# A new order of loads, units and fillers for the first batch of a fused retention and Fourier-mixing kernel

## The chip, the cores and the metric

The kernel runs on one core of a Trainium2 chip. The metric is the device time of one execution in microseconds (us). The names of the engines follow the profile: PE is TensorE, DVE is VectorE, ACT is ScalarE, POOL is GpSimd, SP is SyncE, which only issues DMAs here.

## What is computed

Cut to what matters:

```python
# q, k, v: (4, 8, 768, 64); gamma_h = 1 - 2**(-5 - h)
for t in range(768):                       # retention, for each batch and head
    state = gamma * state + outer(k[t], v[t])
    y[t] = (1 / 8) * q[t] @ state
x = y of all 8 heads side by side          # (4, 768, 512)
u = x + real(fft(fft(x, axis=1), axis=2))
un = (u - mean(u)) / sqrt(var(u) + 1e-6)   # over the 512 features
out = u + relu(un @ w_ch1) @ w_ch2         # 512 -> 2048 -> 512
```

## The kernel before

The four batches are worked through one after the other. A batch's retention is done for four pairs of heads, i = 0 to 3, in chunks of 128 rows. The Fourier transforms are products with tables of cosines and sines (csp, ssp, csn, ssn over the 768 rows, cd and sd over the 512 features), after the halves of x have been folded onto each other. Then come the norm, two products with weights and the store.

For batches 1 to 3 the code gives streams of units with the share of a batch at which each starts and ends (TS0, TS1, DM0, DM1, DA0, DA1, LD0, LD1, HT0), sorts all units by those shares and emits them. The long products there are `psh` (un with w_ch1, L1057) and `psc` (ht with w_ch2, L1100); between them stand the retention and the transforms of the next batch. ACT_ROWS says which of the 16 relus of a row block are done by ACT; the others are DVE's. The loads of batch 1 wait until the seventh of eight weight loads has landed (`load_unit(1, i, 6)`).

The first batch is written out by hand: the string FIRST names the units in order, each with the engine that does it where there is a choice (@a ACT, @v DVE, @g POOL), and `pin()` keeps that order on every engine. An engine that waits for one unit therefore holds all its later ones. For a pair i the units are:

- q`i` (cast of q on POOL), k`i0`/k`i1` (scaled casts of k, one for each head), v`i0` or v`i1` and v`i2` (cast of v, whole or in halves);
- t`i0`, t`i1` (transposes of q and k on PE), e`i0`, e`i1` (their copies out of PSUM);
- am`i0`, am`i1` (products of q and k, each for both heads), ae`i`+half+head (their mask, DVE);
- kv`i` (products of k and v), gk`i` (a table of decays for the scan), sc`i` (the scan over chunks, DVE);
- yi`i`+head, yx`i` (products to y), x`i`+head (y scaled into x), fs`i` (fold: a sum and a difference, DVE, L736), xs`i` (a row sum).

ts, tsa and ta make the tables, fl2 to fl4 mirror parts of them, csn copies the cosines into another order, par makes parity masks. s`e`+block+side are the transform over rows (L803), ge its copies out of PSUM, gr reversed copies of those, g0 to g2 a small product for column 0, sa the transform over features (L897), nh, n, bn and ua the norm and the copy out. w0 to w7 are the weights' loads, which POOL issues and which turn float32 into float16 on the way (L1114, L1121). The filler units are products whose result nobody reads:

```python
    def filler(n):
        def run():
            for _ in range(n):
                nc.tensor.matmul(wps, wz[:, 0:P], wz, start=True, stop=True)
        return run
```

SP issues the twelve loads of the first batch in the order of LOADS0; they share the DMA engines and land one after the other. After FIRST the first product with w_ch1 (`h0`, L1074) starts.

Of the kernel before, what the change touches and what calls it, by code (L numbers as in the profile page):

```python
# [28 lines left out]
MAGIC = 12582912.0  # L29
PAIR_ORDER = [0, 1, 3, 2]  # L30
ORD0 = [1, 0, 3, 2]
LOADS0 = [("q", 0), ("k", 0), ("v", 0), ("q", 1), ("k", 1), ("v", 1), ("q", 2), ("k", 2),
          ("q", 3), ("k", 3), ("v", 2), ("v", 3)]
FIRST = """
tsa2@g tsa0@v ts0 q0 ta00 ta01 ta02 xe1 k01@a k00@a ts2 tsa4@v fill6 t00 e00@a tsa3@g fill5 t01
v00@g e01@a fill4 am00 am01 ts3 ta20 ts4 ta32 ta42 par tsa1@g ts1 gk0 ta10 ae001 ta11 ta12 kv0
q1 fill3 t10 e10@a k10@g sc0 ae011 k11@g yi01 t11 fl4@v ae000 ae010 e11@a yi00 yx0 am10 x00@v
ae100 edge x01@a am11 v10@g q2 kv1 ta40 ta21 ae110 gk1 sc1 k20@g t20 k21@a fill3 t21 e20@a q3
e21@a yi10 ta22 ae101 ae111 yi11 ta30 yx1 am20 gk2 k31@g fs0 s010 v21@g am21 t30 x11@v k30@a
ae201 gk3 e30@a ae211 x10@v t31 e31@a ae210 fill4 am30 am31 ta41 w0 ae200 v32@g v22@v ae300 kv2  # L40
# [11 lines left out]
DA0, DA1 = (-0.023, 0.102, 0.152, 0.211, 0.309, 0.318), (0.053, 0.062, 0.102, 0.166, 0.240, 0.187)  # L52
LD0, LD1 = (0.112, 0.312), (-0.333, 0.129)
HT0 = (0.691, 0.686, 0.693, 0.540)
NPE = 2
ACT_ROWS = ((5, 6, 7, 8, 9, 10, 13, 14), (0, 3, 6, 9, 12, 14, 15), (2, 4, 5, 7, 8, 10, 14))


@with_exitstack
def kernel(  # L60
# [9 lines left out]
    nc = tc.nc  # L70
    gam = [1.0 - 2.0 ** (-5.0 - h) for h in range(H)]
# [37 lines left out]
    gk2 = const.tile([P, NHP], f32, tag="gk2")  # L109
    gk5 = const.tile([P, 2, D, NCH - 1], f32, tag="gk5")  # L110
# [6 lines left out]
    tails, base = {}, {}  # L117
# [43 lines left out]
    wz = ht16[:, 0:2, :].rearrange("p a b -> p (a b)")[:, 0:DM]  # L161
    wps = ps_w.tile([P, DM], f32, tag="w", name="wps")

    def filler(n):
# [2 lines left out]
                nc.tensor.matmul(wps, wz[:, 0:P], wz, start=True, stop=True)  # L167
# [60 lines left out]
    for h in range(H):  # L228
# [4 lines left out]
                            scalar2=float(math.log(0.125)), op0=ALU.mult, op1=ALU.add)  # L233
    nc.vector.tensor_scalar(out=gexp[:, 1], in0=lgrow, scalar1=icol[:, 5:6], scalar2=None,
                            op0=ALU.mult)
    nc.scalar.activation(gexp, gexp, AF.Exp, bias=0.0, scale=1.0)
    for h2 in range(2):
        nc.scalar.activation(gk2[D * h2:D * h2 + D], lgrow[D * h2:D * h2 + D, h2:H:2], AF.Exp,
                             bias=0.0, scale=float(P))
# [3 lines left out]
                            pattern=[[1, P]], channel_multiplier=-1)  # L243
# [9 lines left out]
    def gk_unit(i):  # L253
        def run():
            hp = ORD0[i]
            nc.gpsimd.tensor_copy(gk5[:, i % 2, :, 1:], gk2[:, hp:hp + 1].unsqueeze(
                1).to_broadcast([P, D, NCH - 2]))
        return run

    def late_consts():  # L260
        with tc.issue_after(lb[0]["una"].ins):
# [74 lines left out]
            return trig(idx, S, KN, icol[:, idx:idx + 1], icoln[:, idx:idx + 1])  # L336
        return trig(idx, DM, 257, icol[:, idx:idx + 1], icoln[:, idx:idx + 1])

    def csn_unit():
        for c in range(3):  # L340
            nc.gpsimd.tensor_copy(csn[:, c].rearrange("p (i t) -> p t i", t=2),
                                  csp[:, 0:2, c, 0:192])

    ssn = fp.tile([P, 2, 3, NK], f16, tag="eo", name="ssn", padded_shape=[P, 2, 6, 256])

    def flip_unit(n, eng):
        e = {"v": nc.vector, "g": nc.gpsimd}[eng]
        out, in0, m = ((ssn, ssp, -1.0), (cd16[:, :, 257:512], cd16[:, :, 255:0:-1], 1.0),
                       (sd16[:, :, 257:512], sd16[:, :, 255:0:-1], -1.0))[n - 2]

        def run():
            e.tensor_scalar(out=out, in0=in0, scalar1=m, scalar2=1.0, op0=ALU.mult,
                            op1=ALU.mult)
        return run

    def t_act(idx, part):
# [151 lines left out]
                                     start=True, stop=True)  # L508
        return run

    def ae_unit(i, half, h2):
        def run():
            st = at[0, i]
            nc.vector.scalar_tensor_tensor(  # L514
                out=st["atm"][:, 3 * half:3 * half + 3, h2, :], in0=st["wk", half][h2],
                scalar=float(gam[2 * ORD0[i] + h2] ** (-P)),
                in1=maskf.unsqueeze(1).to_broadcast([P, 3, P]), op0=ALU.mult, op1=ALU.mult)
# [250 lines left out]
    def xsum_unit(i, eng):  # L768
        def run():
            if i == 0:  # L770
                fd[0]["xm"] = stt.tile([P, 4], f32, tag="xm", name="xm")
                fd[0]["mu"] = stt.tile([P, 4], f32, tag="mu", name="mu")
            h = 2 * ORD0[i]
            src = xts[0][:, 0, 0, 64 * h + 1:64 * h + 129] if h < 4 else \
                xts[0][:, 0, 1, 386 - 64 * h:514 - 64 * h]
            if eng == "a":
                junk = ht16[:, 2, 0:P]
                nc.scalar.activation(junk, src, AF.Copy, bias=0.0, scale=1.0,
                                     accum_out=fd[0]["xm"][:, i:i + 1])
            else:  # L780
                nc.vector.tensor_reduce(out=fd[0]["xm"][:, i:i + 1], in_=src, op=ALU.add,
                                        axis=mybir.AxisListType.X)
        return run
# [114 lines left out]
                                 stop=part == 3, skip_group_check=True)  # L898
        return run

    def ua_unit(kb):
        def run():
            nc.vector.tensor_scalar(out=lb[0]["u"][:, kb], in0=lb[0]["pq", kb],
                                    scalar1=fd[0]["g0"][:, kb:kb + 1], scalar2=0.0, op0=ALU.add,
                                    op1=ALU.add)
        return run

    def n0_unit(half, eng):
# [18 lines left out]
            nc.vector.bn_aggr(stats[:, kb, 0:2], bst)  # L927
        return run

    def n_unit(kb):  # L930
        def run():
            un = lb[0]["un", kb] = up.tile([P, 2, 257], f16, tag="un16", name="un16").rearrange(
                "p a b -> p (a b)")[:, 0:DM]
            lb[0]["una"] = nc.scalar.activation(un, lb[0]["u"][:, kb], AF.Identity,
                                                bias=lb[0]["st"][:, kb, 0:1], scale=-1.0)
        return run

    def pt0_unit(half):
# [219 lines left out]
    def first_unit(name):  # L1158
        name, _, eng = name.partition("@")
        kind = name.rstrip("0123456789")  # L1160
        n = [int(c) for c in name[len(kind):]]
        if kind == "tsa":
            return trig_of(n[0])[0](eng or "v")
        if kind == "ts":
            return trig_of(n[0])[1]
        if kind == "ta":
            return t_act(*n)
        if kind == "k":
            return k0_unit(n[0], n[1], eng or "g")
# [24 lines left out]
        plain = dict(csn=csn_unit, mean=mean_unit, edge=edge_zeros)  # L1194
        if kind in plain:
            return plain[kind]
        return dict(gk=gk_unit, q=q0_unit, t=t0_unit, am=am_unit, ae=ae_unit, kv=kv0_unit,
                    sc=sc_unit, yi=yi_unit, yx=yx_unit, fs=fold_p,
                    s=s1b_unit, sa=sa_unit, ua=ua_unit, bn=bn_unit, n=n_unit, pt=pt0_unit,
                    gr=gr_unit, xe=x_edges)[kind](*n)  # L1200

    def mix_units(b, kbs):
# [92 lines left out]
```

## Time and profile before

| | us |
|---|---|
| Median of 3 runs (247.56 to 248.1) | 247.84 |
| The profiled execution itself | 248.4 |
| Its span, first to last instruction | 246.7 |
| PE busy / DVE busy / ACT busy / POOL busy | 234.6 / 184.3 / 113.3 / 86.4 |
| First h0 product starts | 34.54 |
| Start and length of the last output copy | 243.42, 0.35 |

Times within an execution count from the start of the span. The profiled execution lies 0.56 us above the median and has 1.7 us outside the span.

### The profile page before, as it was taken

What the parts mean: (1) busy time and instruction counts of PE and PEld (TensorE: products, weight loads), DVE (VectorE), ACT (ScalarE), POOL (GpSimd) and SP (SyncE); (2) the same over time, 40 slices, a digit from 0 to 9 for tenths busy, and PEclk for the clock granted to TensorE, in tenths of its full rate; (3) what the DMA queues carried; (4) which work ended last, traced back from release to release, by engine and by line L of the source; (5) the groups of instructions that cost most, each with busy time, mean ns of one, the idle gap of its engine ahead of it and who ended that gap; (6) DMA issues with size and microseconds to landing.
All of it is one profiled execution on the core that took longest, in us unless ns stands there. A gap on an engine that the chain in (4) does not pass through costs nothing.

```text
span 246.7 us, 5319 instructions
## 1 busy us (share of the span) xinstructions
PE 234.6 (95%) x2033; PEld 144.5 (59%) x2033; DVE 184.3 (75%) x438; ACT 113.3 (46%) x248; POOL 86.4 (35%) x156
## 2 busy tenths in 40 slices
PE   6988899999999999999999999999999999999994
PEld 2465578956676645765567446655666455445543
DVE  8989897887899788996887738977897657425321
ACT  6986438586864444751236414732245316202300
POOL 8965921454700068590000726660002305000000
PEclk9999999999999999999999999999999999999999
DMA  7995999999999389998999487594200331221012
GB/s 168 254 263 94 193 167 207 230 232 238 300 231 222 74 170 146 217 183 153 253 267 219 83 153 203 115 142 116 88 0 3 71 121 21 45 85 43 0 45 86
DMA packets 99209, 36.39 MB, mean 148 GB/s; under 512 B 89840, under 2 KB 96240, under 8 KB 99184
## 3 DMA queue, kind: packets, MB, share of 16 engines
q1 hardware_dynamic: 94960, 31.86, 61.5%
q0 software_dynamic: 4224, 4.19, 10.6%
q8 instruction: 16, 0.26, 0.5%
q14 instruction: 9, 0.07, 0.1%
HBM read 27.26 MB, written 6.29 MB: 136 GB/s over the span
## 4 chain that ended last, share of the span: by engine, by line
PE 59%; DVE 13%; DMA 9%; POOL 8%; SPq 4%; ACT 3%; issue 3%; POOLq 0%; ACTq 0%; DVEq 0%
PE psh L1057 23%; PE psc L1100 22%; DMA k<-in_k_dram 5%; SPq L201 3%; DVE bst L1019 3%; POOL u L1008 3%; PE wkA L640 3%; PE ps L823 3%; DMA unT<-un 2%; DMA kT<-kd 2%; POOL kd L423 2%; POOL u L1006 1%; PE wkY L694 1%; DVE atm L514 1%; DVE ht L1083 1%
## 5 line engine op out<-in xcount | busy, mean ns | idle before, releaser
L1100 PE MATMUL psc<-w,ht 128*128 128x512 f16 (+2 forms) x400 | 88.9, 370 | 0.0
L1057 PE MATMUL psh<-unT,w 128*128 128x384 f16 x448 | 82.3, 326 | 1.1 <-DMA unT<-un 0.5
L1100 PEld LDWEIGHTS <-ht 128*128 128x128 f16 x400 | 37.5, 98 | 36.7
L1057 PEld LDWEIGHTS <-w 128*128 128x128 f16 x448 | 42.0, 98 | 25.5 <-issue 2.7
L1006 POOL TENSOR_TENSOR u<-u,x 128x256 f32<-128x256 f32 x21 | 13.4, 636 | 104.8 <-DVE u L985 91.4
L1061 ACT ACTIVATE ht<-psh 128x384 f16<-128x384 f32 x51 | 24.7, 489 | 45.2 <-PE psh L1057 45.0
L1063 DVE TENSOR_SCALAR ht<-psh 128x384 f16<-128x384 f32 x61 | 33.0, 550 | 8.6 <-PE psh L1057 8.0
L1104 DVE SCALAR_TENSOR_TENSOR ob<-psc,stats,u 128x512 f32<-128x512 f32 (+2 forms) x25 | 18.1, 725 | 23.4 <-PE psc L1100 23.4
L643 DVE TENSOR_TENSOR atm<-wkA,maskp 128x512 f16<-128x512 f32 x36 | 23.8, 684 | 2.9 <-PE wkA L640 2.8
L1021 ACT ACTIVATE un<-u,stats 128x512 f16<-128x512 f32 x21 | 15.2, 722 | 17.8 <-DVE stats L1020 14.2
L669 DVE SCALAR_TENSOR_TENSOR s<-s,gk,wkK 128x128 f16<-128x128 f16 x48 | 16.3, 340 | 4.6 <-ACT s L665 3.5
L1019 DVE BATCH_NORM_STATS2 bst<-u 128x6 f32<-128x512 f32 x21 | 14.6, 693 | 6.2 <-POOL u L1008 6.1
L702 ACT ACTIVATE x<-wkY,gexp 128x384 f16<-128x384 f32 x24 | 12.7, 582 | 9.9 <-PE wkY L694 9.9
L423 POOL TENSOR_SCALAR kd<-k,gexp 128x384 f16<-128x384 f32 x24 | 13.8, 588 | 3.5 <-DMA k<-in_k_dram 3.5
L1008 POOL TENSOR_TENSOR u<-u,x 128x256 f32<-128x256 f32 x21 | 13.4, 636 | 4.2 <-DVE stats L1020 3.0
L640 PE MATMUL wkA<-qTz,kT 128*128 128x256 f16 x72 | 13.1, 273 | 0.4 <-DMA kT<-kd 0.4
L1074 PE MATMUL psh<-unT,w 128*128 128x128 f16 x192 | 11.4, 219 | 0.7 <-ACT unT L950 0.3
L1074 PEld LDWEIGHTS <-w 128*128 128x128 f16 x192 | 11.0, 98 | 1.2 <-issue 1.2
L980 ACT COPY qn<-pq 128x128 f32<-128x128 f32 x18 | 4.9, 275 | 14.6 <-PE pq L978 14.4
L167 PE MATMUL wps<-ht 128*128 128x512 f16 x31 | 9.4, 447 | 2.1 <-POOL ht L226 2.1
L428 POOL TENSOR_SCALAR v<-v 128x768 f16<-128x768 f32 x12 | 10.0, 835 | 1.8 <-DMA v<-in_v_dram 1.6
L640 PEld LDWEIGHTS <-kT 128*128 128x128 f16 x72 | 6.8, 98 | 5.9 <-DMA kT<-kd 0.9
(175 smaller groups left out, 325.6 us busy)
## 6 DMA issues: line engine op xcount, KB each, us to landing
q<-in_q_dram SPq DMA_DIRECT2D x16, 384.0 KB, 6.0
k<-in_k_dram SPq DMA_DIRECT2D x16, 384.0 KB, 5.6
v<-in_v_dram SPq DMA_DIRECT2D x16, 384.0 KB, 6.4
out_dram<-ob SPq DMA_DIRECT2D x23, 256.0 KB, 2.4
w<-in_moe_w_ch_dram POOLq DMA_DIRECT2D x8, 512.0 KB, 9.6
unT<-un SPq DMA_TRANSPOSE x15, 2.4
out_dram<-ob SPq DMA_DIRECT2D x1, 192.0 KB, 1.9
qTz<-q16z SPq DMA_TRANSPOSE x8, 4.6
```

The source lines that it names most:

```text
L423: kc = nc.gpsimd.tensor_scalar(out=kd[:, :, h2, :], in0=k32[:, h2], scalar1=gkd[:, h0 + h2:h0 + h2 + 1], scalar2=1.0, op0=ALU.mult, op1=AL ...
L640: mm = nc.tensor.matmul(wk[:, c2], st["kT"][:, c, :], st["qT"][:, :, c, :], start=True, stop=True)
L643: nc.vector.tensor_tensor(out=st["atm"][:, 2 * part:2 * part + 2], in0=wk, in1=maskp[:, PAIR_ORDER[i]].unsqueeze(1).to_broadcast([P, 2, 2, ...
L669: nc.vector.scalar_tensor_tensor(out=s16[:, c], in0=s16[:, c - 1], scalar=gk2[:, hp:hp + 1], in1=wk[:, c - c0], op0=ALU.mult, op1=ALU.add)
L1008: nc.gpsimd.tensor_tensor(out=u[:, kb, 256:512], in0=u[:, kb, 256:512], in1=x[:, kb, 1, 257:1:-1], op=ALU.add)
L1019: nc.vector.bn_stats(bst, u[:, kb, :])
L1057: nc.tensor.matmul(psh, w116[:, cb, fb * P:(fb + 1) * P], unT[:, cb, rt * 384:(rt + 1) * 384], start=(cb == 0), stop=(cb == 3))
L1061: nc.scalar.activation(ht16[:, fb, :], psh, AF.Relu, bias=0.0, scale=-1.0)
L1063: nc.vector.tensor_scalar(out=ht16[:, fb, :], in0=psh, scalar1=-1.0, scalar2=0.0, op0=ALU.mult, op1=ALU.max)
L1074: mm = nc.tensor.matmul(psh[:, f], w116[:, cb, fb * P:(fb + 1) * P], unT[:, cb, kb * P:(kb + 1) * P], start=(cb == 0), stop=(cb == 3))
L1100: nc.tensor.matmul(psc[:, c0:c1], ht16[:, fb, rb3 * P:(rb3 + 1) * P], w216[:, fb, c0:c1], start=(fb == 0), stop=(fb == NFB - 1))
L1104: nc.vector.scalar_tensor_tensor(out=ob[:, c0:c1], in0=psc[:, c0:c1], scalar=lb[b]["st"][:, rb, 3:4], in1=lb[b]["u"][:, rb, c0:c1], op0=AL ...
```

## The change

The order of FIRST and LOADS0 is new. The kinds of units that can choose an engine are more: gk (ACT or POOL), csn (split into three copies, each on ACT, POOL or DVE), fl (ACT as well), ua (ACT or DVE), n and ae (the choice is there, but not used otherwise than before). A new filler `long` does products of float32 with 256 columns. The 25 filler products in FIRST become 2 of the old kind and 8 of float32; the 6 ahead of FIRST stay. The shares of the later turns and ACT_ROWS have new values. What later batches compute is the same.

```diff
-LOADS0 = [("q", 0), ("k", 0), ("v", 0), ("q", 1), ("k", 1), ("v", 1), ("q", 2), ("k", 2),
-          ("q", 3), ("k", 3), ("v", 2), ("v", 3)]
+LOADS0 = [("q", 0), ("k", 0), ("q", 1), ("k", 1), ("v", 0), ("k", 2), ("v", 1), ("q", 2), ("v",
+          2), ("q", 3), ("k", 3), ("v", 3)]
 FIRST = """
-tsa2@g tsa0@v ts0 q0 ta00 ta01 ta02 xe1 k01@a k00@a ts2 tsa4@v fill6 t00 e00@a tsa3@g fill5 t01
-v00@g e01@a fill4 am00 am01 ts3 ta20 ts4 ta32 ta42 par tsa1@g ts1 gk0 ta10 ae001 ta11 ta12 kv0
-q1 fill3 t10 e10@a k10@g sc0 ae011 k11@g yi01 t11 fl4@v ae000 ae010 e11@a yi00 yx0 am10 x00@v
-ae100 edge x01@a am11 v10@g q2 kv1 ta40 ta21 ae110 gk1 sc1 k20@g t20 k21@a fill3 t21 e20@a q3
-e21@a yi10 ta22 ae101 ae111 yi11 ta30 yx1 am20 gk2 k31@g fs0 s010 v21@g am21 t30 x11@v k30@a
-ae201 gk3 e30@a ae211 x10@v t31 e31@a ae210 fill4 am30 am31 ta41 w0 ae200 v32@g v22@v ae300 kv2
-sc2 s110 fl2@g yi21 yi20 ae310 ta31 fs1 yx2 v31@a x20@a w1 w2 s100 s000 ae311 ae301 kv3 yi31
-x21@a fs2 s001 sc3 s101 yi30 yx3 fl3@g x31@v ge00@a ge10@a x30@a fs3 gr2 xs0@a xs3@v csn w3
-sa00 sa10 sa11 g0 s011 s111 ge01@a xs1@v ge11@v gr0 sa20 sa02 sa01 sa03 g1 xs2@a mean sa22
-nh0@v g2 nh1@a sa12 pt0 gr3 sa13 ua0 sa21 pe0@a ua1 sa23 pt1 pe1@a gr1 bn1 ua2 w4 w5 w6 w7 bn2
-n1 n2
+k00@a k01@a tsa0@v ts0 xe1 tsa4@g gk1@a q0 long1 t00 tsa2@v ts2 ta02 e00@a tsa1@g ts4 t01
+tsa3@g ts1 ta00 e01@a ta10 ta22 v00@g par@v q1 gk0@g k10@v k11@a ta12 long3 am00 am01 ta42 ta11
+k20@g ae010@v ae001@v long2 kv0 ae000@v ae011@v t10 sc0 t11 e10@a yi01 v10@g yi00 yx0 e11@a
+long1 am10 q2 x01@a am11 ts3 ta32 ta20 x00@v ta01 fl4@g ae101@v ae100@v k21@a kv1 long1 t20
+ta21 e20@a ae111@v yi11 t21 sc1 ae110@v yi10 fs0 fl2@g yx1 q3 s110 k31@g e21@a x10@v am20 am21
+x11@a fs1 ta40 v22@a s010 k30@a t30 e30@a fill1 t31 v21@g e31@a ae201@v ta30 ae200@v kv2
+ae211@v yi21 ae210@v gk2@g sc2 csn2@a w0 w1 csn1@v fill1 am30 ae300@v ta31 yi20 yx2 v32@g x20@a
+ae301@v xs0@v x21@a ta41 fl3@a gk3@g s100 am31 ae311@v s000 v31@g kv3 fs2 s101 ge10@a ae310@v
+w2 s001 w3 yi31 sc3 ge00@a yi30 yx3 g0 x30@a sa00 sa10 edge x31@v fs3 w4 gr0 sa11 csn0@v s011
+xs2@a xs3@v w5 s111 xs1@a sa20 mean ge01@a sa02 sa01 ge11@v sa03 nh0@a gr3 sa12 nh1@a gr1 sa13
+g1 sa21 pt0 g2 ua1@v pt1 sa22 pe0@a pe1@a w6 ua0@v bn1 sa23 ua2@a gr2 n1 bn2 n2 w7
 """
-DM0, DM1 = (0.101, 0.194, 0.248, 0.334), (-0.003, 0.131, 0.160, 0.383)
-TS0 = (0.282, 0.345, 0.387, 0.439, 0.487, 0.518, 0.675, 0.686)
-TS1 = (-0.032, -0.002, 0.042, 0.582)
+DM0, DM1 = (0.121, 0.179, 0.253, 0.368), (0.004, 0.137, 0.232, 0.341)
+TS0 = (0.269, 0.376, 0.393, 0.441, 0.517, 0.575, 0.665, 0.696)
+TS1 = (-0.040, -0.020, 0.048, 0.585)
...
-LD0, LD1 = (0.112, 0.312), (-0.333, 0.129)
-HT0 = (0.691, 0.686, 0.693, 0.540)
+LD0, LD1 = (0.160, 0.263), (-0.370, 0.140)
+HT0 = (0.683, 0.767, 0.685, 0.583)
-ACT_ROWS = ((5, 6, 7, 8, 9, 10, 13, 14), (0, 3, 6, 9, 12, 14, 15), (2, 4, 5, 7, 8, 10, 14))
+ACT_ROWS = ((2, 5, 6, 7, 8, 9, 10, 14), (0, 3, 6, 7, 9, 10, 11, 12, 14, 15), (2, 4, 5, 6, 7, 8, 10, 14))
...
+    wz32 = wz.bitcast(f32)
+
+    def filler32(n):
+        def run():
+            for _ in range(n):
+                nc.tensor.matmul(wps[:, 0:256], wz32[:, 0:P], wz32, start=True, stop=True)
+        return run
...
-    def csn_unit():
-        for c in range(3):
-            nc.gpsimd.tensor_copy(csn[:, c].rearrange("p (i t) -> p t i", t=2),
-                                  csp[:, 0:2, c, 0:192])
+    def csn_unit(c, eng):
+        copy = {"a": nc.scalar.copy, "g": nc.gpsimd.tensor_copy, "v": nc.vector.tensor_copy}[eng]
+        return lambda: copy(csn[:, c].rearrange("p (i t) -> p t i", t=2), csp[:, 0:2, c, 0:192])
```

More of the change, by code (lines that the diff above doesn't have):

```diff
@@ L48 @@
 FB = 1
-DM0, DM1 = (0.101, 0.194, 0.248, 0.334), (-0.003, 0.131, 0.160, 0.383)
-TS0 = (0.282, 0.345, 0.387, 0.439, 0.487, 0.518, 0.675, 0.686)
-TS1 = (-0.032, -0.002, 0.042, 0.582)
-DA0, DA1 = (-0.023, 0.102, 0.152, 0.211, 0.309, 0.318), (0.053, 0.062, 0.102, 0.166, 0.240, 0.187)
-LD0, LD1 = (0.112, 0.312), (-0.333, 0.129)
-HT0 = (0.691, 0.686, 0.693, 0.540)
+DM0, DM1 = (0.121, 0.179, 0.253, 0.368), (0.004, 0.137, 0.232, 0.341)
+TS0 = (0.269, 0.376, 0.393, 0.441, 0.517, 0.575, 0.665, 0.696)
+TS1 = (-0.040, -0.020, 0.048, 0.585)
+DA0, DA1 = (0.034, 0.100, 0.173, 0.180, 0.306, 0.315), (0.063, 0.067, 0.063, 0.158, 0.168, 0.189)
+LD0, LD1 = (0.160, 0.263), (-0.370, 0.140)
+HT0 = (0.683, 0.767, 0.685, 0.583)
 NPE = 2
-ACT_ROWS = ((5, 6, 7, 8, 9, 10, 13, 14), (0, 3, 6, 9, 12, 14, 15), (2, 4, 5, 7, 8, 10, 14))
+ACT_ROWS = ((2, 5, 6, 7, 8, 9, 10, 14), (0, 3, 6, 7, 9, 10, 11, 12, 14, 15), (2, 4, 5, 6, 7, 8, 10, 14))
 @with_exitstack
@@ L251, with gk_unit @@
     nc.vector.tensor_copy(kf, kf_i)
[L253 to L258, printed above, removed]
+    def gk_unit(i, eng):
+        copy = nc.scalar.copy if eng == "a" else nc.gpsimd.tensor_copy
+        hp = ORD0[i]
+        return lambda: copy(gk5[:, i % 2, :, 1:], gk2[:, hp:hp + 1].unsqueeze(1).to_broadcast(
+            [P, D, NCH - 2]))
     def late_consts():
@@ L337, in trig_of @@
         return trig(idx, DM, 257, icol[:, idx:idx + 1], icoln[:, idx:idx + 1])
-    def csn_unit():
-        for c in range(3):
-            nc.gpsimd.tensor_copy(csn[:, c].rearrange("p (i t) -> p t i", t=2),
-                                  csp[:, 0:2, c, 0:192])
+    def csn_unit(c, eng):
+        copy = {"a": nc.scalar.copy, "g": nc.gpsimd.tensor_copy, "v": nc.vector.tensor_copy}[eng]
+        return lambda: copy(csn[:, c].rearrange("p (i t) -> p t i", t=2), csp[:, 0:2, c, 0:192])
     ssn = fp.tile([P, 2, 3, NK], f16, tag="eo", name="ssn", padded_shape=[P, 2, 6, 256])
     def flip_unit(n, eng):
-        e = {"v": nc.vector, "g": nc.gpsimd}[eng]
         out, in0, m = ((ssn, ssp, -1.0), (cd16[:, :, 257:512], cd16[:, :, 255:0:-1], 1.0),
@@ L351, in run @@
         def run():
-            e.tensor_scalar(out=out, in0=in0, scalar1=m, scalar2=1.0, op0=ALU.mult,
-                            op1=ALU.mult)
+            if eng == "a":
+                nc.scalar.activation(out, in0, AF.Copy, bias=0.0, scale=m)
+            else:
+                (nc.gpsimd if eng == "g" else nc.vector).tensor_scalar(
+                    out=out, in0=in0, scalar1=m, scalar2=1.0, op0=ALU.mult, op1=ALU.mult)
         return run
@@ L509, in am_unit, with ae_unit @@
         return run
-    def ae_unit(i, half, h2):
+    def ae_unit(i, half, h2, eng):
         def run():
             st = at[0, i]
[L514 to L517, printed above, removed]
+            dst, src = st["atm"][:, 3 * half:3 * half + 3, h2, :], st["wk", half][h2]
+            scale = float(gam[2 * ORD0[i] + h2] ** (-P))
+            if eng == "a":
+                nc.scalar.activation(dst, src, AF.Copy, bias=0.0, scale=scale)
+                nc.gpsimd.affine_select(out=dst, in_=dst, compare_op=ALU.is_ge, fill=0.0, base=0,
+                                        pattern=[[0, 3], [1, P]], channel_multiplier=-1)
+            else:
+                nc.vector.scalar_tensor_tensor(
+                    out=dst, in0=src, scalar=scale,
+                    in1=maskf.unsqueeze(1).to_broadcast([P, 3, P]), op0=ALU.mult, op1=ALU.mult)
         return run
@@ L899, in sa_unit, with ua_unit @@
         return run
-    def ua_unit(kb):
+    def ua_unit(kb, eng):
         def run():
-            nc.vector.tensor_scalar(out=lb[0]["u"][:, kb], in0=lb[0]["pq", kb],
-                                    scalar1=fd[0]["g0"][:, kb:kb + 1], scalar2=0.0, op0=ALU.add,
-                                    op1=ALU.add)
+            dst, src, g0 = lb[0]["u"][:, kb], lb[0]["pq", kb], fd[0]["g0"][:, kb:kb + 1]
+            if eng == "a":
+                nc.scalar.activation(dst, src, AF.Identity, bias=g0, scale=1.0)
+            else:
+                nc.vector.tensor_scalar(out=dst, in0=src, scalar1=g0, scalar2=0.0, op0=ALU.add,
+                                        op1=ALU.add)
         return run
@@ L928, in bn_unit, with n_unit @@
         return run
-    def n_unit(kb):
+    def n_unit(kb, eng):
         def run():
@@ L933, in run @@
                 "p a b -> p (a b)")[:, 0:DM]
-            lb[0]["una"] = nc.scalar.activation(un, lb[0]["u"][:, kb], AF.Identity,
-                                                bias=lb[0]["st"][:, kb, 0:1], scale=-1.0)
+            src, mu = lb[0]["u"][:, kb], lb[0]["st"][:, kb, 0:1]
+            if eng == "a":
+                lb[0]["una"] = nc.scalar.activation(un, src, AF.Identity, bias=mu, scale=-1.0)
+            else:
+                lb[0]["una"] = nc.vector.tensor_scalar(out=un, in0=src, scalar1=-1.0, scalar2=mu,
+                                                       op0=ALU.mult, op1=ALU.add)
         return run
@@ L1189, in first_unit @@
             return xsum_unit(n[0], eng or "v")
+        if kind == "long":
+            return filler32(n[0])
         if kind == "fill":
@@ L1193, in first_unit @@
             return w1_unit(n[0]) if n[0] < 4 else w2_unit(n[0] - 4)
-        plain = dict(csn=csn_unit, mean=mean_unit, edge=edge_zeros)
+        if kind == "ae":
+            return ae_unit(*n, eng or "v")
+        if kind == "csn":
+            return csn_unit(n[0], eng or "g")
+        if kind == "gk":
+            return gk_unit(n[0], eng or "g")
+        if kind == "ua":
+            return ua_unit(n[0], eng or "v")
+        if kind == "n":
+            return n_unit(n[0], eng or "a")
+        plain = dict(mean=mean_unit, edge=edge_zeros)
         if kind in plain:
             return plain[kind]
-        return dict(gk=gk_unit, q=q0_unit, t=t0_unit, am=am_unit, ae=ae_unit, kv=kv0_unit,
+        return dict(q=q0_unit, t=t0_unit, am=am_unit, kv=kv0_unit,
                     sc=sc_unit, yi=yi_unit, yx=yx_unit, fs=fold_p,
-                    s=s1b_unit, sa=sa_unit, ua=ua_unit, bn=bn_unit, n=n_unit, pt=pt0_unit,
+                    s=s1b_unit, sa=sa_unit, bn=bn_unit, pt=pt0_unit,
                     gr=gr_unit, xe=x_edges)[kind](*n)
```

## The prediction

> **What bounds the kernel now.** I read the windows first, then the chain of waits, then the timelines of the first batch. The windows from 40 to 240 us (length, then busy us of PE, weight loads, DVE, ACT, POOL):
>
> ```profile
> 40.00:240.00 200.00, 197.24 (x1595) 119.90 (x1593) 146.86 (x347) 86.80 (x193) 60.16 (x98) 1.00 0.68 141
> ```
>
> PE idles 2.76 us in 200, and its work there stays the same: later turns can win 2.76 at most. The first batch is the other place. Its chain (start, length, what):
>
> ```profile
> 9.73 5.55 DMA k<-in_k_dram
> ...
> 22.82 0.82 DVE s L538
> 23.64 0.45 DVE atm L514
> 24.09 1.78 DVE xab L736 x2
> 25.87 0.93 DVE atm L514 x2
> 26.80 1.17 DVE xab L736 x2
> ```
>
> From 22 to 28 us DVE's work ends last, and two of its pieces are long. The timeline of DVE and POOL tells why:
>
> ```profile
> 17.62 0.64 DVE L736 TENSOR_TENSOR xab<-x 128x387 f16<-128x387 f16 x2
> 23.79 1.17 POOL L352 TENSOR_SCALAR ssn<-ssp 128x1158 f16<-128x1158 f16 x1
> 24.01 1.86 DVE L736 TENSOR_TENSOR xab<-x 128x384 f16<-128x384 f16 x2
> 26.72 1.24 DVE L736 TENSOR_TENSOR xab<-x 128x384 f16<-128x384 f16 x2
> 27.03 1.92 POOL L341 COPY csn<-csp 128x384 f16<-128x384 f16 x3
> 29.64 0.62 DVE L578 TENSOR_SCALAR x<-wkY,gexp 128x384 f16<-128x384 f32 x1 [0.96 <-PE wkY L561]
> 30.36 0.63 DVE L736 TENSOR_TENSOR xab<-x 128x384 f16<-128x384 f16 x2
> ```
>
> A fold (two instructions) takes 0.64 by itself, 1.86 beside POOL's mirror ssn, 1.24 beside POOL's csn.
>
> **The change, step by step.** Positions are from the built order of both programs, times from rows of before.
>
> *Loads.* In the trace q0, k0, v0, q1, k1 land at 4.21, 6.02, 7.75, 8.91, 10.69: a q takes 1.15, a k or v 1.75; all twelve end at 21.4. In the new order I get q1 7.2, k1 8.9, v0 10.7, k2 12.4, v1 14.1, q2 15.3, v2 17.0, q3 18.2, k3 19.9 and v3 21.6.
>
> *Pairs 0 and 1.* On ACT k00 and k01 now stand first and wait for k0 (6.05); with the rows' starts 0.5 apart for k, 0.7 for e, 0.4 to 0.5 for a table step, e01 ends at 9.9 (before 9.66). POOL casts v0 to 11.5, then q1, which stands behind it, to 12.35, then gk0 to 12.75 (0.83, 0.83, 0.40). So sc0 starts at 12.8 instead of 11.14. But DVE does pair 0's four masks first, ends sc0 at 13.6, and yx0 comes at 13.9, as before. am10 follows at about 15.2: DVE starts pair 1's masks 0.2 later than in before (14.99).
>
> *DVE from there to the end of fs3* (before 31.0, so 16.0 long). It loses the cast v22 (0.55) and x11 (0.62), which go to ACT; fl2 is now done about 17 to 18 and csn no longer by POOL, so fs1 and the later fold fall to 0.64 each: 1.22 and 0.60 less. It gains csn1 (no row of DVE; bounds 0.25, the gr copy of 128x384 on DVE, and 0.55, the float32 cast; I take 0.3, nearer the f16 copy) and xs0, 0.28. The two xg instructions (0.5) move into the 0.96 wait for yx3: nothing; without that wait 0.5. Folds fs0 and fs1 now stand beside POOL's casts of q3, k3 and v2: 0 to 1.2 (the excess of the 1.86 row), taken at 0.4, because the 17.62 fold ran its 0.64 beside the end of a POOL copy. Sum: -0.55 -0.62 -1.82 +0.3 +0.28 +0.4 = -2.0; with the later start, fs3 ends 1.8 earlier, at 29.2. What could be late next is ACT, which has more to do: e31 ends by my rows at 22.5, and DVE wants am30 at 23.5, so there is 1.0 of cover; whatever e31 is later than 23.5 comes straight off the gain. kv3 needs v3's cast, now behind k3, v2, gk2 and two weight issues on POOL: 24.6, and sc3 stands at 26.5 at the earliest.
>
> The Trainium skill's page "SBUF — State Buffer", section "Who interferes with whom", says that a Vector instruction with two SBUF inputs and a GpSimd instruction that reads SBUF exclude each other for a whole instruction. The 1.86 row agrees. By that rule fs0 and fs1 would pay nearer 1.2 than 0.4, and the gain shrinks by 0.8.
>
> *Tail.* gr0, csn0 and xs3 now lie between fs3 and ge11: 0.25 + 0.3 + 0.28 against 0.95 for the products s011 and s111, so ge11 is some 0.2 later after fs3 than before. ua2 on ACT costs 0.72 by the row of un (same shape) and takes as much off DVE, behind nh and pe; fl3 on ACT 0.61, before x30, in ACT's idle time; gk1 on ACT 0.4 to 0.5, within the wait for q0. k10 on DVE (0.5) stands before am00 is ready. These cost nothing where they stand.
>
> *Fillers.* 25 old products become 2 old and 8 of float32 with 256 columns. The rows of old ones:
>
> ```profile
> 2.15 4.48 PE L167 MATMUL wps<-ht 128*128 128x512 f16 x12 [2.15 <-POOL ht L226]
> 20.53 1.03 PE L167 MATMUL wps<-ht 128*128 128x512 f16 x4
> ```
>
> Starts are 0.43 apart until 5.54, 0.22 later. For a float32 product there is no row: between 0.11 (256 columns at the late pace) and 1.7 (four times 0.43). I take 0.43, two late old ones, near the geometric middle. Only the three in a row before am00 are close to the path: t01 ends at 7.7, kT is ready at 9.9, so they cost nothing below 0.73 each. The single one before am10 adds up to 0.4. I put 0.2 for fillers in all.
>
> The Trainium skill's page "FP8 and Floating Point Precision", section "TensorE Precision Notes", has float32 in four passes; an estimate from it and the rows is 0.43 late and 0.85 early. No run here shows it yet.
>
> *Weights.* w0 is issued behind k31, v21 and gk2 on POOL: 19.9 + 0.6 + 0.5 + 0.4 = 21.4, before 22.29. Landings 2.6 apart follow: w3 at 36.7 instead of 37.6. The product that needs it starts at 38.74 and moves to 37.2: still covered, by 0.5.
>
> *Batch 1.* Its loads start when w6 lands (45.2, then 45.4 the first load): 0.85 earlier, less than the PE's 1.5. PE waited there already:
>
> ```profile
> 62.77 0.51 PE L596 MATMUL tq<-ident,kd 128*128 128x128 f16 x6 [0.36 <-POOL kd L423]
> ```
>
> With the new shares four more psc products (0.87) stand before this transpose: 62.41 + 0.87 - 1.5 = 61.8 against k ready at 61.9. So the gain survives; without the four products 0.8 of it would go.
>
> *Later turns.* PE's order differs by shifts of 4 to 12 products; SP's order is nearly the same, so the waits for DMA transposes stay possible. Bounds: -2.76 and +2.76; I take 0, since a shift removes waits and makes others.
>
> Sum: -1.8 +0.2 +0.2 = -1.4. On the profiled execution: 248.4 - 1.4 = 247.0. It lies 0.56 over the median: 246.4.
>
> **Rivals.**
>
> 1. *The later turns pay as well.* Half of the 2.76 goes: 245.0. For it: some waits in the batches are for a DVE relu, and ACT now has more of the relus. Against: DMA waits are untouched.
> 2. *The gain is taken back at batch 1.* If SP's loads or the weights start as late as before, PE waits at the transposes of pairs 2 and 3 for what it gained: about 247.7. For it: the wait of 0.36 above. Against: w0 goes out earlier.
> 3. *PE stays at the slow pace (slower).* Starts 0.43 apart for the first 3.4 us of unbroken work, then 0.22. After the change PE has holes at 6.0 to 7.2 and 9.0 to 9.9. If the pace stays slow to 15 us, PE's work from 10 to 15 (4.01 busy less 0.65 of fillers, plus three float32 products, 1.3) takes 9.4 instead of 4.7; of these 4.7 some 1.6 fall in holes, and the other 3.1 against the gain of 1.4 give 247.84 + 1.7 = 249.5. It decides from a float32 price of 0.73 or a slow pace past 9 us. Against it: fillers still stand in every hole over 1 us but one. The Trainium skill's page "TensorE: Matmul & The Clock Gate", Part 1, says that the clock doubles after about 3.4 us of sustained activity and falls back only after an idle window as long. The rows' change at 5.54, after a start at 2.15, agrees. By that rule this rival fails unless the first window is missed.
> 4. *The new turns make new waits (slower).* 2.76 more, less the 1.4: 249.2. For it: batch 1's steps 2 to 5 move by up to 0.057 of a batch, some 3 us, towards their successors. Against: batch 1's folds and row transform stand where they stood among the psc products of batch 0.
>
> **Numbers.** A measurement of this kernel tells about 0.2%, 0.5 us. Forecast 0.45 (245.3 to 247.3), rival 1 0.13, rival 2 0.12 (0.10 of it within 0.5 us), rival 3 0.15, rival 4 0.15. Faster 0.45 + 0.13 + 0.02 = 0.60, same 0.10, slower 0.30. The range leaves out the far half of rival 1 and the upper parts of rivals 3 and 4: 244.8 to 249.2. For the forecast alone, 245.3 to 247.3.
>
> **What would show it.** Right: the fold that stood at 24.01 takes 0.64; fs3 ends near 29.2; the first h0 product starts near 33.0 (34.54 before); w3 lands by 37; PE idles about 2.8 us between 40 and 240. Wrong: float32 products of over 0.73; starts of the PE's products at half pace after 6 us; folds fs0 and fs1 over 1.5; e31 ending after 23.5; or PE idle of over 4 us after 40.

## The result, and the profile after

The changed kernel takes 246.33 us (median of 4 runs, 246.14 to 246.58); the kernel before, beside it on the same chip, 247.74 (4 runs, 247.56 to 248.1). The ratio is 0.9942, 95% interval 0.9925 to 0.9959: 1.4 us faster, the amount forecast. The profiled execution took 246.58 us, its span is 244.3.

The total agrees, but its parts don't. The windows from 40 to 240 us, as before the change (length, then busy us of PE, weight loads, DVE, ACT, POOL):

```profile
40.00:240.00 200.00, 198.04 (x1598) 120.98 (x1598) 139.13 (x332) 90.78 (x202) 60.09 (x98) 1.00 0.70 142
```

PE idles 1.96 us there, 0.80 less than before; DVE has 7.7 us less to do, ACT 4.0 more. The forecast had this idle time unchanged.

The chain of waits up to batch 1 (start, length, what):

```profile
13.73 7.56 DMA k<-in_k_dram
...
21.37 0.58 POOL kd L460
21.96 0.47 POOL v L472
22.43 0.34 POOL gk L264
22.77 0.93 POOL w L1135
...
28.88 16.28 DMA w<-in_moe_w_ch_dram
...
50.26 5.32 DMA k<-in_k_dram
...
55.73 1.16 POOL kd L431 x2
...
56.94 0.51 PE tq L610 x6
```

Before, the first batch's chain ran through DVE's folds and masks from 22 to 28. Now it hangs on a load, k3, which lands at 21.28; POOL's cast of it (k31), v21, gk2 and the weights' issues stand in a row behind it. The weights then set when batch 1's loads start, and PE waits for the second of their k casts at 56.94. The timeline of DVE (start, length, operation, and in brackets the idle time before it with its releaser; "..." marks lines left out):

```profile
19.33 0.64 DVE L750 TENSOR_TENSOR xab<-x 128x384 f16<-128x384 f16 x2
...
23.07 0.82 DVE L552 TENSOR_TENSOR_SCAN s<-gk,wkK 128x320 f16<-128x320 f32 x1 [1.25 <-PE wkK L543]
23.81 0.86 DVE L348 COPY csn<-csp 128x384 f16<-128x384 f16 x1
...
26.46 0.62 DVE L750 TENSOR_TENSOR xab<-x 128x384 f16<-128x384 f16 x2
...
29.69 0.63 DVE L750 TENSOR_TENSOR xab<-x 128x384 f16<-128x384 f16 x2
```

The folds (L750) are short, as forecast: 0.62 to 0.64 where 1.86 and 1.24 stood. But the scan sc2 starts after 1.25 us of waiting for kv2, which k3 holds up, and fs3 ends at 30.32, not at 29.2 (before: 30.99). h0 starts at 34.06 (before 34.54), the first `psc` product at 47.33 (48.43), and the last output copy ends at 241.75 (243.77). So 0.5 us comes in the first batch, another 0.6 up to the first `psc`, and 0.9 later. (Of the 2.0, some 0.4 is the choice of executions: the one profiled before lies 0.66 over its median, this one 0.25 over; another 0.2 is lost behind the last copy, from whose end the execution runs 4.63 us before and 4.83 now.) PE's first products in this kernel:

```profile
4.68 1.06 PE L175 MATMUL wps<-ht 128*128 128x256 f32 x2
6.11 0.51 PE L489 MATMUL tq<-ident,q16z 128*128 128x128 f16 x6 [0.37 <-POOL q16z L446]
...
7.55 1.51 PE L175 MATMUL wps<-ht 128*128 128x256 f32 x6
```

A float32 product is two records. Three products are x6, whose records start some 0.226 us apart, so one product costs 0.45.

### The profile page after: what moved, and what is told of

Same layout as the page of the kernel before. It is cut to its first block, busy times and chain, and to the rows that moved or that the text cites. A ratio compares the mean times of both kernels' runs of the same rounds, so it can differ in the third digit from the quotient of the medians.

```text
span 244.3 us, 5306 instructions
## 1 busy us (share of the span) xinstructions
PE 233.1 (95%) x2026; PEld 145.8 (60%) x2026; DVE 174.3 (71%) x423; ACT 121.4 (50%) x268; POOL 83.1 (34%) x151
## 4 chain that ended last, share of the span: by engine, by line
PE 69%; DMA 14%; POOL 6%; SPq 5%; DVE 3%; issue 1%; ACT 1%; POOLq 0%; ACTq 0%
PE psc L1121 31%; PE psh L1078 25%; DMA w<-in_moe_w_ch_dram 7%; DMA k<-in_k_dram 5%; SPq L209 5%; PE wkA L654 3%; PE ps L837 3%; PE wkY L708 2%; DMA q<-in_q_dram 2%; PE wkY L704 1%; PE pq L999 1%; POOL w L1135 1%; PE wkK L673 1%; DVE u L1006 1%; POOL u L1027 1%
## 5 line engine op out<-in xcount | busy, mean ns | idle before, releaser
L1082 ACT ACTIVATE ht<-psh 128x384 f16<-128x384 f32 x64 | 30.9, 489 | 40.3 <-PE psh L1078 39.7
L1084 DVE TENSOR_SCALAR ht<-psh 128x384 f16<-128x384 f32 x48 | 26.1, 548 | 8.6 <-PE psh L1078 8.2
L716 ACT ACTIVATE x<-wkY,gexp 128x384 f16<-128x384 f32 x24 | 12.8, 580 | 9.9 <-PE wkY L708 9.9
L1006 DVE SCALAR_TENSOR_TENSOR u<-pq,g,qn 128x256 f32<-128x256 f32 x18 | 8.5, 472 | 3.1 <-PE psh L1078 2.5
```

The source lines that it names most:

```text
L1082: nc.scalar.activation(ht16[:, fb, :], psh, AF.Relu, bias=0.0, scale=-1.0)
L1084: nc.vector.tensor_scalar(out=ht16[:, fb, :], in0=psh, scalar1=-1.0, scalar2=0.0, op0=ALU.mult, op1=ALU.max)
```

## Experiments

Ratios are to the kernel before, run beside it on the same chip; h0, the first `psc` and the end of the last output copy (us) are from the profiled execution.

| kernel | median us | ratio, 95% interval | h0 | first psc | last copy ends |
|---|---|---|---|---|---|
| changed | 246.33 | 0.9942 (0.9925 to 0.9959) | 34.06 | 47.33 | 241.75 |
| 1 changed, old shares and rows | 247.37 | 0.9989 (0.9976 to 1.0001) | 34.13 | 47.38 | 242.13 |
| 2 before, new shares and rows | 248.06 | 1.0017 (1.0001 to 1.0033) | 34.97 | 49.39 | 244.06 |
| 3 changed, kv2 ahead | 245.63 | 0.9918 (0.9903 to 0.9933) | 33.58 | 46.84 | 240.81 |
| 4 changed, no fillers | 245.49 | 0.9914 (0.9894 to 0.9934) | 33.33 | 46.59 | 240.63 |
| 5 both 3 and 4 | 245.64 | 0.9925 (0.9895 to 0.9954) | 33.64 | 46.91 | 240.81 |
| 6 changed, f16 fillers | 246.11 | 0.9943 (0.9921 to 0.9965) | 33.97 | 47.23 | 241.20 |
| 7 before, no fillers | 247.99 | 1.0021 (0.9994 to 1.0048) | 35.49 | 49.38 | 242.81 |
| 8 changed, csn on POOL | 246.82 | 0.9974 (0.9959 to 0.9989) | 34.23 | 47.21 | 242.82 |
| 9 changed, old TS0 and TS1 | 247.73 | 0.9989 (0.9973 to 1.0005) | 34.29 | 47.55 | 243.30 |
| 10 as 3, old middle row of ACT_ROWS | 246.60 | 0.9937 (0.9915 to 0.9959) | 33.63 | 46.91 | 241.94 |
| 11 changed, k3 ahead of v2 | 245.83 | 0.9933 (0.9912 to 0.9953) | 33.74 | 47.00 | 241.10 |

**1 and 2: first batch alone, shares alone.** In 1 all of DM, TS, DA, LD, HT and ACT_ROWS of the changed kernel are those of before; in 2 they are put, new, into the kernel before.

> The changed kernel with the shares of the later turns (DM, TS, DA, LD, HT) and ACT_ROWS of before; FIRST, LOADS0 and the unit choices stay new. In the traces the first psc product comes 1.1 us earlier (48.43 to 47.33), and PE idles 0.8 us less between 40 and 240. Theory A, both parts pay: the first batch alone gives 1.1 less what batch 1's later loads take back, so 0.4 to 1.0 us under before (ratio 0.996 to 0.9985), first psc near 47.3. Rival B, the first batch pays it all: ratio 0.994. Rival C, without the new shares PE waits at the transposes of batch 1 for all that it gained: ratio 0.999 to 1.001, with a wait of over 1.2 us at one of these transposes.

> The kernel before with only the shares of the later turns and ACT_ROWS of the change. Theory A: 0.4 to 0.9 us under before (ratio 0.9965 to 0.9985), PE's idle time from 40 to 240 near 2.0 instead of 2.76. Rival B: ratio 1.000. Rival C, the shares only make sense with the earlier first batch: with the old one PE waits nowhere at the transposes of batch 1, and the time is 1.000 to 1.002 of before.

The first batch alone reaches the first `psc` as early as the whole change (47.38), and yet its time can't be told from before. The shares alone are 0.2% slower, at the edge of what can be told. So the gain is not a sum of two gains: the new first batch pays only with shares that use it.

Where kernel 1 loses the gain, its trace doesn't show. Its ratio is that of rival C, but the wait of over 1.2 isn't there: the first three k transposes of batch 1 wait 0.41, 0.29 and 0.22, and the last copy ends only 0.4 later than in the changed kernel, in an execution of 247.07, one of the two shortest of twelve. In kernel 2 PE waits at none of these three transposes, as its rival C has it; it idles 2.74 us from 40 to 240, not near 2.0. Its h0 comes 0.4 later than before although FIRST is the same: in this execution PE's granted clock, the share of its full speed that the chip allows, is half from 15.71 to 19.12.

**9: which shares.**

```diff
-TS0 = (0.269, 0.376, 0.393, 0.441, 0.517, 0.575, 0.665, 0.696)
-TS1 = (-0.040, -0.020, 0.048, 0.585)
+TS0 = (0.282, 0.345, 0.387, 0.439, 0.487, 0.518, 0.675, 0.686)
+TS1 = (-0.032, -0.002, 0.042, 0.582)
```

> The changed kernel with only TS0 and TS1 as before: 16, 32, 44 psc products ahead of batch 1's first three k transposes. Theory T: PE waits 0.9 to 1.5 us at them and the time is 247.0 to 247.5. Rival U: no more wait than in the changed kernel, 246.2 to 246.5.

With the old steps the ratio is that of kernel 1. The timeline of PE in kernel 9, at the first and the third of batch 1's transposes of k:

```profile
52.46 0.51 PE L610 MATMUL tq<-ident,kd 128*128 128x128 f16 x6 [0.51 <-POOL kd L431]
...
62.33 0.51 PE L610 MATMUL tq<-ident,kd 128*128 128x128 f16 x6 [0.24 <-POOL kd L431]
```

PE gets to both before k's cast. Counted from start to start, less the time of the product before, the two gaps are 0.67 and 0.40, together within the 0.9 to 1.5 expected; with the new steps there is one, 0.75 at 56.94, so that these transposes cost only 0.3 more. Later the old steps also wait 0.53 at 95.0 for v's cast, 0.65 at 156.9 and 0.38 at 165.1, while a wait of 0.84 at 93.7 for ACT's un, which comes with the new steps, falls to 0.26: together 1.0 more. The time rises by 0.47% of 248, 1.2 us, and 247.73 lies above the 247.0 to 247.5 of theory T. So the old steps do cost the gain, but most of it is lost later than at the transposes that T names. The mirror image, old shares with the new TS0 and TS1, took 249.15 us (ratio 1.0047, 1.0028 to 1.0066), but that mixture of orders computes something else, and its time answers nothing.

> The changed kernel with the old shares and ACT_ROWS, as in the run with old shares (247.37), but with the new TS0 and TS1. In the built order that puts 24, 32, 48 psc products ahead of batch 1's first three k transposes, as the change does, instead of 16, 32, 44. Theory T (the place of these transposes is what the first batch's gain needs): the waits there sum to under 0.8 us and the time is within 0.3 of the changed kernel's 246.3. Rival U (the gain needs the other shares or the rows of ACT): 247.2 or more, with the waits at the later turns.

**10: the rows of ACT.**

```diff
-ACT_ROWS = (..., (0, 3, 6, 7, 9, 10, 11, 12, 14, 15), ...)
+ACT_ROWS = (..., (0, 3, 6, 9, 12, 14, 15), ...)
```

> The changed kernel with kv2 ahead (as in the run with kv2 ahead, 245.63) and with the middle tuple of ACT_ROWS as before: seven of the sixteen relus on ACT instead of ten. It tests one of the later turns by itself. Theory R (ten rows make ACT late with un, which PE awaits 0.84 us at 93): that wait falls to 0.3 to 0.5, DVE's busy time rises by 3 to 6 us without PE waiting for it, 245.2 to 245.5. Rival V (the rows were moved for DVE's sake): new PE waits for DVE of 0.4 or more, 245.6 to 246.2.

My theory R fell: the wait for un at 93.6 stays 0.84, so ten rows on ACT are not its cause. DVE is busier by 5.6 us between 40 and 240, as expected, and new short waits come (the weight load of a tile that DVE masks, then a product behind a late relu of ACT):

```profile
76.44 0.17 PEld L708 LDWEIGHTS <-atm 128*128 128x128 f16 x4 [0.37 <-DVE atm L657]
...
76.91 1.30 PE L1078 MATMUL psh<-unT,w 128*128 128x384 f16 x7 [0.17 <-ACT ht L1082]
```

Rival V doesn't fit either: from start to start PE waits 0.28 there for DVE, less than its 0.4, and 246.60 lies above its 245.6 to 246.2. The last copy ends 1.13 later than in kernel 3 and the median is 0.97 higher, but by the ratios it is 0.5, and their intervals overlap. That the new rows are part of the gain of the later turns is likely, not shown.

**3 and 11: k3 and the wait of the scan.** In 3, v21 and gk2 stand ahead of k31 on POOL, and kv2 ahead of t31 on PE. In 11, the load k3 goes ahead of v2, and ACT's v22 behind e30.

```diff
-... q3 s110 k31@g e21@a ...        ... t31 v21@g e31@a ... kv2 ... gk2@g sc2
+... q3 s110 v21@g gk2@g k31@g e21@a ...   ... kv2 t31 e31@a ... sc2
```

> The changed kernel with v21 and gk2 moved ahead of k31 on POOL, and kv2 ahead of t31 on PE. In the changed kernel DVE waits 1.25 us at sc2 (23.07) for kv2, which waits for v21 and so for k31, whose load lands at 21.28. Theory A: that wait is the step that kept fs3 from 29.2: sc2 starts at 21.8, am30 (ready 23.45) then sets the masks, fs3 ends 0.8 to 1.2 earlier than 30.3, the first h0 product 0.6 to 1.2 earlier than 34.06, and 0.3 to 1.0 us of it stay in the time (ratio to before 0.990 to 0.993). Rival B: ACT's e31, which waits for the same load, sets the masks and everything behind: fs3 moves by under 0.3 and the time stays at 0.994. Rival C: fs3 moves, but the weights (w3 lands at 37.06, used at 37.28) hold PE: h0's fourth group stays at 37.2, ratio 0.994.

> The changed kernel with load k3 ahead of v2, as in the kernel before (q3, k3, v2, v3), and ACT's cast v22 behind e30. Theory L (the wait of 1.25 us of sc2 comes of the load order: k3 is the eleventh load and takes the 1.3 us of the late packet, and k31, v21, the k transposes and kv2 follow it one after the other): k3 lands at 18.3 to 19.6, v2 at 21.3, kv2 needs only v2's cast, sc2 starts at 22.3 to 22.6 instead of 23.07, h0 at 33.4 to 33.7; w0's issue stays at 22.6 to 22.8 since v21 and gk2 still stand ahead of it; 245.7 to 246.1. Rival M (whichever load comes late, sc2 waits as long): sc2 at 23.0 or later, 246.3 or more.

The timeline of DVE in kernel 3, and in kernel 11:

```profile
22.18 0.80 DVE L552 TENSOR_TENSOR_SCAN s<-gk,wkK 128x320 f16<-128x320 f32 x1
...
23.86 1.02 DVE L529 SCALAR_TENSOR_TENSOR atm<-wkA,maskf 128x384 f16<-128x384 f32 x2 [0.61 <-PE wkA L515]
```

```profile
22.87 0.82 DVE L552 TENSOR_TENSOR_SCAN s<-gk,wkK 128x320 f16<-128x320 f32 x1 [0.46 <-PE wkK L543]
```

In 3 the wait of 1.25 is gone, w0 is issued at 21.94 instead of 22.71, and the median falls to 245.63, within theory A. But fs3 ends at 29.83 and h0 starts at 33.58, each 0.5 earlier, where A had 0.8 to 1.2 and 0.6 to 1.2: DVE now waits for am30, which stands behind ACT's e31 and the same late load, so rival B holds in part. In 11 k3 lands at 18.41 and v2 takes the delay (21.52); 0.46 of the wait stays, since kv2 needs v2's casts. The scan is 0.27 later and h0 0.04 later than I expected, the time is within what I expected. Both point to the same thing: the late load and what is queued behind it are a part of what the first batch lost against the forecast. Of the 1.06 between 33.0 and 34.06, kernel 3 brings back 0.48 and kernel 11 0.32; kernel 4, below, 0.73.

**4, 5, 6, 7: the fillers.** 4 and 5 leave out the ten filler products of FIRST, 7 the 25 of the kernel before; 6 has two f16 products for each float32 one. All compute what they did, since nobody reads a filler.

> The changed kernel without the eight float32 and two other filler products in FIRST (the six ahead of FIRST stay); nothing of the result is lost. Theory A, they only fill waits: time within 0.3 us of the changed kernel (ratio to before 0.993 to 0.996), starts of the transposes and masks unmoved. Rival D, they keep PE at its fast pace: without them transposes and products after 6 us run at half pace (starts of a group of six transposes 0.107 apart instead of 0.067 or so), the first h0 product comes 1 to 4 us later, and the time is 0.3 to 2.5 us over the changed kernel (ratio 0.995 to 1.004).

> The changed kernel with both earlier edits: no fillers in the first batch, and v21, gk2 ahead of k31 on POOL with kv2 ahead of t31 on PE. Theory F (the late fetch of PE instructions is what the fillers cost; both edits cure the same wait of 1.25 us of sc2 for k3's chain): the 16 KB packet goes at about 19.2, k3 lands near 20.1, sc2 doesn't wait, and the two gains (0.70 and 0.84 us) do not add: 245.3 to 245.6, h0 33.2 to 33.4. Rival G (they are separate gains): h0 near 32.8, 244.8.

> The changed kernel with each float32 filler product written as two f16 ones of 512 columns (18 fillers in all). Theory F: what counts is how many records PE runs before 17.5 us, and a float32 product is two records of 0.226 us, the same as two f16 ones, so nothing moves: packet at 17.4 to 17.6, k3 at 21.3, 246.3 +-0.3. Rival H (float32 products cost or gain something of their own, by their pace or by the state of the clock): more than 0.5 us away, with other starts of am10 and sc0.

> The kernel before without its 25 fillers in the first batch. Theory F: the packet goes at 19 or later instead of 17.4, so the eleventh load (v2) lands near 20.1 instead of 21.4; the gain is smaller than in the changed kernel, since DVE's long folds (1.86 and 1.24) set the end there and not a wait for a load: 247.0 to 247.7. Rival S (the fillers keep PE's pace up and the kernel before needs them, its PE being on the chain earlier): half pace until 20 us, h0 a microsecond later, 248.5 or more.

Kernel 4 fits neither of its theories: it is 0.8 us faster than the changed kernel, where A allowed 0.3 and D had a loss. Kernel 7's 247.99 lies between the ranges of its two (247.0 to 247.7, and 248.5 or more).

What makes one load late can be read from the trace's records of DMA packets. On the queue for instructions there are 16 packets of 16 KB in the whole execution; the page counts them, and PE's instructions, in these lines:

```profile
PE 233.1 (95%) x2026; PEld 145.8 (60%) x2026; DVE 174.3 (71%) x423; ACT 121.4 (50%) x268; POOL 83.1 (34%) x151
...
q8 instruction: 16, 0.26, 0.5%
```

That is one packet for every 253 PE records (twice 2026 over 16). The first one, and the load that came later than 1.15 (a q) or 1.75 (a k or v) after the one ahead of it, by 1.2 to 1.4 us, v3 by 0.7:

| kernel | packet starts, lasts (us) | PE records before it | late load |
|---|---|---|---|
| before | 17.40, 1.30 | 276 | v2, 21.42 |
| changed | 17.50, 1.13 | 266 | k3, 21.28 |
| 6 f16 fillers | 17.20, 1.06 | 255 | q3, 19.56 |
| 11 k3 ahead | 17.53, 1.30 | 261 | v2, 21.52 |
| 4 no fillers | 19.20, 1.29 | 260 | v3, 22.55 (k3 at 20.07) |
| 7 before, no fillers | 19.23, 1.29 | 240 | v3, 22.58 (v2 at 20.10) |

All of them fit one account: after some 240 to 280 records PE's next instructions are fetched, the packet holds one of the sixteen DMA engines that the loads share, and a load in flight lands late. Which load that is doesn't follow from the packet's start alone: in kernels 1, 8 and 10 (17.06, 17.54, 17.30) it is q3, in 3 and 9 (17.48, 17.66) k3, as in the changed kernel; k3 lands between 21.2 and 21.5 in all of these. Leaving out fillers moves the packet to 19.2, where it hits v3, for which nobody waits in kernel 4. Two f16 fillers are as many records as one float32 product, and kernel 6 is like the changed one. That the packet is PE's own, and that it holds one engine, is inferred from these counts and sizes; that it comes later without fillers, and that v3 instead of k3 or v2 is then the late load, is shown. In kernel 5 the edits of 3 and 4 together bring no more than each alone, as two cures of the same wait would. But its 33.64 for h0 is 0.2 later than I expected: fs0 and fs1 lay beside POOL's work and took 1.28 and 0.98 (0.83 and 0.64 in the changed kernel), which can hide a part of what the two would add.

The fillers also do what they are for. The timeline of PE in kernel 4, where the products of 7.23 and 17.76 are of the same form as those at 21.15:

```profile
6.12 0.82 PE L489 MATMUL tq<-ident,q16z 128*128 128x128 f16 x6 [1.23 <-POOL q16z L446]
7.23 0.82 PE L489 MATMUL tq<-ident,kd 128*128 128x128 f16 x6 [0.29 <-ACT kd L458]
9.77 0.82 PE L515 MATMUL wkA<-qTz,kT 64*128 64x128 f16 x12 [1.73 <-ACT kT L501]
...
17.76 0.83 PE L489 MATMUL tq<-ident,kd 128*128 128x128 f16 x6
...
21.15 0.50 PE L489 MATMUL tq<-ident,q16z 128*128 128x128 f16 x6
```

Six transposes take 0.82 until about 18 us and 0.50 from 20 on, and the trace's record of the full granted clock begins at 19.90; in the changed kernel they take 0.51 from 6.11, and the full clock begins at 5.95. The Trainium skill's page "TensorE: Matmul & The Clock Gate", Part 1, says that the clock opens only after about 3.4 us of sustained activity; here, with holes of 0.3 to 1.7 us between groups at first, that was not met before 19.90. In this kernel the slow pace lies beside DVE's and the loads' time and costs less than the packet at 17.5: 245.49 without fillers against 246.33 with them. In kernel 7 h0 comes 0.96 later, as its rival said, yet the total is only 0.2% higher with an interval that holds 1. Its twelve runs spread from 246.53 to 249.69, and the profiled one has the full clock from 5.11 to 8.52 and then half until 18.76, so whether the kernel before needs its fillers stays open.

**8: the copies beside the folds.**

```diff
-... sc2 csn2@a w0 w1 csn1@v ...   ... s000 v31@g kv3 fs2 ...   ... sa11 csn0@v s011
+... sc2 w0 w1 ...   ... s000 v31@g csn0@g csn1@g csn2@g kv3 fs2 ...   ... sa11 s011
```

> The changed kernel with its three copies csn0 (DVE 0.38), csn1 (DVE 0.86), csn2 (ACT 0.63) back on POOL, in a row ahead of fold fs2, as in the kernel before. Theory C (a fold beside such a POOL copy takes 1.2 to 1.9 instead of 0.62): DVE saves 1.24 by the copies and pays 0.6 to 1.3 in the fold and some in its neighbours; h0 within 0.4 of 34.06, and 246.0 to 246.8. Rival N (no exclusion; the fold's long times had another cause): fs2 stays under 0.7, h0 comes a microsecond earlier, 245.3.

The timelines of DVE and POOL in kernel 8:

```profile
26.02 1.24 DVE L750 TENSOR_TENSOR xab<-x 128x384 f16<-128x384 f16 x2
```

```profile
25.86 1.87 POOL L348 COPY csn<-csp 128x384 f16<-128x384 f16 x3
27.66 1.55 POOL L1135 DMA_DIRECT2D w<-in_moe_w_ch_dram  x2
```

The fold beside POOL's csn takes 1.24 instead of 0.62, the value of the kernel before: this step of the forecast holds. The Trainium skill's page "SBUF — State Buffer", section "Who interferes with whom", says that such a pair excludes each other; this run agrees. But h0 moves by 0.17 only. The loss of 0.3% against the changed kernel comes at batch 1, as far as the profiled execution shows it (247.49, the longest of its twelve): batch 1's first load lands at 50.86 instead of 49.38, and PE waits for a k cast:

```profile
57.75 0.51 PE L610 MATMUL tq<-ident,kd 128*128 128x128 f16 x6 [1.47 <-POOL kd L431]
```

Why that load is late is not shown. The copies delay w2 to w7 by 1.84 at their issue, but w6, on which the loads wait, lands at 44.96 (45.16 in the changed kernel), and the first load is issued at 45.11 (45.31); it takes 5.75 instead of 4.07.

## Why the prediction was right, and where it was not

**Total, and its split.** -1.4 was forecast, -1.4 measured. I had put all of it before h0; there it is -0.5. The trace has -1.5 more from h0 to the last copy, of which 0.4 is the choice of executions and 0.2 is lost again behind that copy; the 0.9 that is left came from terms that I had at nothing. Two errors of like size cancelled, so the agreement of the total is luck.

**Loads: wrong by 1.4 for k3** (19.9; measured 21.28). I counted 1.75 for each k and v, and the trace of before already had v2 at 21.42, 3.1 after k3, where that sum gives 20.0; I took the end of all twelve for 21.4, too, while v3 landed at 22.54. The timeline of POOL before the change has it, at the cast that waits for v2:

```profile
21.49 0.51 POOL L464 TENSOR_SCALAR v<-v 128x384 f16<-128x384 f32 x1 [2.46 <-DMA v<-in_v_dram]
```

This is the step that failed. From it follow e31 (copy ends at 23.40, not 22.5), w0 (22.71, not 21.4), and the wait of 1.25 that my sum for DVE didn't have. Kernels 3, 4 and 11, which end or shorten that wait, bring h0 forward by 0.5, 0.7 and 0.3.

**DVE.** sc0 at 12.79 (12.8) and the masks of pair 1 at 15.13 (15.2) are as worked out, and so are the folds (0.62 and 0.63; fs0 0.83, fs1 0.64: 0.2 of contention where I took 0.4). csn1 was mis-sized: 0.3, measured 0.86. In other kernels it took 0.35 (3), 0.59 (4 and 5) and 0.75 (11); in the longer ones ACT's csn2 and a cast or a weight issue on POOL ran beside it, and which of these costs it wasn't separated. With the wait that is 1.8 too little, less 0.2 for the folds; fs3 was late by 1.1, and I have not split the rest.

**Tail: right.** From fs3's end to h0 it was 3.54 before and is 3.74 now: the +0.2. That ua2 on ACT costs nothing was right, that it brings nothing wasn't: DVE's first relu starts at 36.57 instead of 38.04, PE's waits of 0.51 and 0.44 among the h0 products shrink to 0.2 or less, and 0.6 more is gained up to the first `psc`. No run separates ua2 from the rest of this.

**Fillers: price right** (0.43; 0.45), and rival 3 fell, since the pace holds from 6 us. Where it doesn't hold, its price was too high: in kernel 9's execution, with the same first batch, the full clock begins only at 11.05, and h0 comes 0.2 later. The rule that I took for the clock's fall, only after an idle stretch of some 3.4 us, is not what kernel 2 shows: its clock falls at 15.71 after 3.41 us in which PE was busy for 2.41, with no hole over 0.5. What I hadn't seen is that fillers also hasten the packet: without the ten of FIRST the kernel is 0.8 us faster.

**Batch 1: right that the gain needs the new shares, wrong in where.** The loads don't start 0.85 earlier (45.31; 45.37 before), and pair 1's transpose waits 0.75, which I had not forecast. Without the new shares, or without the new steps alone, the gain goes: by their ratios kernels 1 and 9 are both 1.2 us slower than the changed one, where I had 0.8. But I had that at the transposes of batch 1, and there kernel 1 waits only 0.2 more than the changed kernel and kernel 9 only 0.3 more. Rival 2 as I described it shows in kernel 8 alone.

**Later turns: I took 0.** 0.8 of the 2.76 went, as rival 1 has it in part; whether for its reason, relus on ACT, kernel 10 leaves likely and not shown. One new wait came (un, 0.84), as rival 4 has it, but others went: 0.69 at 147.3 and 0.60 at 165.6 for DMA transposes, against which I had argued.

**A version that beats both.** Kernels 3, 4 and 5 are 0.75 to 0.86% below the kernel before, by their medians 0.7 to 0.8 us below the changed one, and not to be told from each other. They were not run beside the changed kernel, and the intervals of the ratios overlap with its own.

## What to carry to other kernels

Forecast landings from the trace's own landings, load by load: a gap of 3.1 among gaps of 1.75 is a term, not an outlier, and it stays while the loads move past it. A gain in a prologue can be lost in the order of what consumes it; test the two parts singly before adding them up. Moving work off a DMA-issuing engine can pay at the neighbour that it blocked (the fold of kernel 8), and letting it issue sooner moves the transfers behind it: in kernel 3 w0 goes out 0.77 earlier and batch 1's loads start 0.92 earlier.

## What the runs showed of the hardware that was not expected

- The packets of 16 KB on the queue for instructions take 0.9 to 1.6 us each in the kernels before and changed, one for some 253 PE records, and a load in flight at the first lands 0.7 to 1.4 us late. A product that does nothing still brings the next packet nearer: 17.50 with the ten fillers, 19.20 without.
- Without fillers PE ran at half pace until 19.90 us (0.82 instead of 0.50 for six transposes), though its holes were all under 1.8 us.
- The clock can fall to half without a long hole (kernel 2, from 15.71 to 19.12). That execution's mean granted clock is recorded as 0.993; so it is in 14 of the 80 runs of the kernel before beside the experiments (median 248.28 us, the others 247.50), and in none of the kernels with the new FIRST and its fillers. What this adds to the gain of the change has not been separated.
- A float32 product of 256 columns is recorded as two products and two weight loads, 0.45 us in all, the time of two f16 ones of 512 columns.
